# Clearing the operands of batch 0's attention on VectorE ahead of it, and making the offset mask behind it

## The chip, the core and the metric

The kernel runs on one core of one Trainium2 chip. The core has five engines with a queue of instructions each: TensorE (PE, matrix products), VectorE (DVE), ScalarE (ACT), GpSimd (POOL) and SyncE (SP), which here issues the DMAs. The metric is the device time of one execution in microseconds: 973.74 us, the median of three runs (971.68 to 973.83).

## The reference

Attention over 8 batches, 8 heads, 576 positions and 64 channels, in two parts that are added, and then a feed-forward layer over the 4608 rows that come out. All is float32.

```python
def _attn_ref(q, k, v):
    factor = 4
    q_d, k_d, v_d = (a.reshape(B, H, S // factor, factor, D).mean(axis=3) for a in (q, k, v))
    out_up = np.repeat(sm_attn(q_d, k_d, v_d), factor, axis=2)     # coarse attention
    mask = np.abs(pos[:, None] - pos[None, :]) < factor            # local attention: 7 offsets
    scores = np.where(mask, scale * np.matmul(q, k.transpose(0, 1, 3, 2)), -1000000000.0)
    ...
    return out_up + np.matmul(attn, v)

def _moe_ref(x, w_in, w_out, s, b):
    r = np.maximum(x @ w_in, 0.0)
    return (s * (r * r) + b) @ w_out
```

`x` is the attention's output with the heads side by side, 4608 x 512; `w_in` is 512 x 2048, `w_out` 2048 x 512. The weights and the scalars come in as 64-bit floating point.

## The kernel before, in words

**Attention.** Work is in units of one batch and one pair of heads, four pairs to a batch; a pair fills the 128 partitions. `first_unit` does a pair of the batches 0 to 2 in one pass: `down` (lines 263 to 331) makes the coarse part (sums of four rows of q and k on VectorE, L271 and L273; sums of v on GpSimd, L282 to L287; scores `sa`, softmax, the transposes `tp` and `tr`, and the product `up`), and around it `first_unit` makes the local part in windows of 32 columns: scores `sl` on top of a mask that TensorE adds from `maskb` (L372 and L377), their maximum and difference on VectorE (L382, L383), the exponential (L386), row sums and reciprocal (L387 to L389), the product with it (L390, on GpSimd for batch 0), a transpose on VectorE (L400), four copies into a block-diagonal operand `bd` (L403), and the products `ol` (L420), to which `up` is added as `x` is written (L423). The batches from 3 on use another form of the local part, `local_unit`, over shifted copies of k and v; this alone reads the offset mask `omask` (L460).

**Block-diagonal operands.** `bd`, and the operands `qc`, `vdr` and `vm` of the coarse part, are zero outside their blocks and are written only in the blocks, so each set is cleared once. One set (`db`, `dq`) serves pair 0 and, later, all other batches. For pairs 1 to 3 of batch 0, which are to overlap with pair 0, there are three more sets, laid in buffers that the weights take later (`make_room`); `clear(i)` zeroes one: 1952 elements a partition in four memsets of 488, and 256 in one more (L186, L187).

**Weights.** `w_in` and `w_out` come in eight parts. `load_w` issues the loads; `split_w` converts each part to a high and a low float32 half (L225 on ScalarE, L226 to L229 on VectorE, L230 on ScalarE, L233 on VectorE).

**Feed-forward.** Rows go in 18 tiles of 256. `split_x` makes a high and a low half of `x` (L530 on ScalarE, L531 on VectorE), `gemm1` does three products for each tile and part (L544 to L546), then relu, square and split (L554 to L557), and `gemm2` three more (L589 to L591).

**What sets the order.** The instructions are emitted in the order of the code. A planner then orders each engine's queue ahead of time: among the instructions that are ready in its own estimate of the times, it takes the one with the lowest number, which is the place in the emission; `tc.high_priority(offset=400)` around the units of batch 0 puts them 400 places ahead. On the chip each engine takes its queue in that order, and waits by semaphores. The accumulators lie in eight tiles (numbers 0 to 7 of `bank`), called banks here; batch 0's units take seven of them in turn (`bk`, line 626), so a later pair's tile waits until an earlier pair's tile in that bank has been read. Ahead of batch 0's units stand, in the emission: the loads of pairs 0 and 1, the identity, `mask` and `maskb`, `omask`, the memsets of `dq` and `db`, `ones` and `eps`, the loads of pairs 2 and 3, the first weights, the two scalars and `clear(1)`; `clear(2)` and `clear(3)` stand ahead of their units.

Of the kernel before, what the change touches and what calls it, by code (L numbers as in the profile page):

```python
# [10 lines left out]
F32 = mybir.dt.float32  # L11
# [7 lines left out]
P = 128  # L19
B, H, S, D = 8, 8, 576, 64  # L20
HP = H // 2
# [20 lines left out]
CH = 9  # L42
NC_ = S // CH
HALO = FAC - 1
NO = 2 * HALO + 1
# [16 lines left out]
def attention_ffn_kernel(ctx, tc, qk, vw_in, vr_in, vdm, qkn, vn, w_in, w_out, s_in, b_in, out):  # L62
    nc = tc.nc
# [39 lines left out]
    def load_pair(b, hp):  # L103
        if (b, hp) in ld:
            return
        own = {}
        if b == 0 and hp:
            room[hp] = make_room(hp)
            own = room[hp]["load"]

        def load(tag, shape, src, pool=one):
            t = own[tag] if tag in own else pool.tile(shape, F32, tag=tag, name="t" + tag)
            nc.sync.dma_start(t, src)
            return t

        tqk = load("qk", [P, 2, SP], qk[b, hp], two)
        tvr = load("vr", [P, FAC, D], vr_in[b, hp])
        tvd = load("vd", [KM, FAC, P], vdm[b, hp])
        tvw = load("vw", [P, NG, P], vw_in[HP * b + hp]) if HP * b + hp < EU else None
        ld[(b, hp)] = (tqk, tvw, tvr, tvd)  # L120
# [13 lines left out]
    def keep(ap, pattern, base, cm):  # L134
        nc.gpsimd.affine_select(
            out=ap, in_=ap, pattern=pattern, compare_op=ALU.is_ge,
            fill=NEG, base=base, channel_multiplier=cm)
# [11 lines left out]
    nc.vector.tensor_copy(maskb[:, 0 : NG : NG - 1], mask[:, 1:3])  # L149


    omask = cst.tile([P, CH, NO], F32, name="omask")
    nc.gpsimd.memset(omask, 0.0)
    for u in range(2):
        mu = omask[64 * u : 64 * u + 64]
        keep(mu, [[1, CH], [1, NO]], -HALO, CH)
        keep(mu, [[-1, CH], [-1, NO]], S - 1 + HALO, -CH)

    dq = cst.tile([P, NQ * 2 * GQ + 3 * P], F32, name="dq")
    nc.vector.memset(dq, 0.0)
    QV = NQ * 2 * GQ + P
# [4 lines left out]
    bias = cst.tile([P, DM], F32, name="bias")  # L168
    eps = cst.tile([P, 1], F32, name="eps")
    nc.gpsimd.memset(eps, 4e-9)  # L170

    db = one.tile([P, 2 * NG, P], F32, tag="big", name="db")
    nc.vector.memset(db, 0.0)
# [8 lines left out]
    def clear(i):  # L182
        da, vm = room[i]["dg"], room[i]["sc"][:, 1536:1792]
        n = 2 * NG * P
        for j in range(0, n + QV, 488):
            nc.gpsimd.memset(da[:, j : min(j + 488, n + QV)], 0.0)  # L186
        nc.gpsimd.memset(vm, 0.0)  # L187
        diag[i] = (take(da, 0, [P, 2 * NG, P]), *blocks(da, n, vm))


# [5 lines left out]
    def load_w(p):  # L196

        parts = (("i", src_i[:, :, 512 * p : 512 * p + 512]), ("o", src_o[:, 2 * p : 2 * p + 2]))
        for op, src in parts:
            st = one.tile([P, 1024, 2], I32, tag=f"w{op}{STAGE[p]}", name="wst")  # L200
            nc.sync.dma_start(st.rearrange("p (k f) t -> p k (f t)", k=src.shape[1]), src)
            wst[(p, op)] = st
# [32 lines left out]
    def split_w(p):  # L235
        with tc.high_priority(offset=-BEHIND.get(p, 0)):
            split_parts(p)
# [377 lines left out]
            load_pair(*units[j])  # L615

    NY = [10 * HP] * NE + [34 * (HP // 2)] * (B - NE)
    for hp in range(2, HP):
        load_pair(0, hp)
    load_w(0)  # L620
    sb_s = cst.tile([P, 1], F32, name="sb_s")
    nc.sync.dma_start(sb_s, bass.AP(s_in.tensor, s_in.offset, [[0, P], [1, 1]]))
    sb_b = cst.tile([P, 1], F32, name="sb_b")
    nc.sync.dma_start(sb_b, bass.AP(b_in.tensor, b_in.offset, [[0, P], [1, 1]]))
    clear(1)
    bk = banks(0, 1, 2, 3, 5, 6, 7)
    for hp in range(HP):
        load_ahead(hp)
        if hp > 1:
            clear(hp)  # L630
        with tc.high_priority(offset=400):
            for _ in first_unit(0, hp, bk):
                pass
    split_w(0)
    load_w(1)
    load_w(2)
# [121 lines left out]
```

## Time and profile before

| | us |
|---|---|
| median of three runs | 973.74 (971.68 to 973.83) |
| time of the profiled execution | 974.94 |
| its span, first to last instruction | 973.1 |
| TensorE busy | 937.4 (96%) |
| VectorE busy | 646.8 (66%) |
| ScalarE busy | 478.8 (49%) |
| GpSimd busy | 425.0 (44%) |

The profile comes from one execution. A row of the order in time has the start, the duration in microseconds, the engine, the line of the code, the operation, what is written and read, the shape, and how many instructions are merged; a bracket gives the idle time of that engine just before and who ended it. A row of a group has the count, the busy time in microseconds, the mean of one in nanoseconds, and the idle time before them. Rows of stages have the busy time of each engine in each stretch with the number of instructions, the granted clock of TensorE (1.00 is full), and the DMA share. Buffers of pairs 1 to 3 of batch 0 are all named `flat`; those of pair 0 have their own names (`dq`, `db`, `pl`, `sm`).

### The profile page before, as it was taken

To read this page: it belongs to the slowest core of one execution; us is meant where nothing else is said; L and a number is where in the kernel's file an instruction comes from. 1 tells how busy PE (TensorE), PEld (TensorE's weight loads), DVE (VectorE), ACT (ScalarE), POOL (GpSimd) and SP (SyncE) were. 2 spreads that over 40 slices of the span, in tenths; PEclk is the share of its full clock that TensorE was granted. 3 is DMA by queue.
4 is the path that set the end of the run, shared out by engine and by line. 5 is a ranking of instruction groups with operands and counts; after the bars stand their busy time and mean duration, and the time that the engine had idled before them with its cause. 6 is when DMAs were issued, how large, how long until landed. Compare 5 with 4: busy or idle time off the path is not lost.

```text
span 973.1 us, 18535 instructions
## 1 busy us (share of the span) xinstructions
PE 937.4 (96%) x7316; PEld 840.0 (86%) x7316; DVE 646.8 (66%) x1175; ACT 478.8 (49%) x1141; POOL 425.0 (44%) x455
## 2 busy tenths in 40 slices
PE   5769999999999999999999999999999999999998
PEld 4558888788999989889989898999899999998997
DVE  5999985864468778878787975876787772211121
ACT  5878775453755454534545344454454444333231
POOL 9422011100167686776767585575776750000000
PEclk9579999999999999999999999999999999999999
DMA  9746422102233232322323232231323100000000
GB/s 314 261 132 204 166 65 73 60 31 86 88 122 112 86 101 85 133 65 72 106 93 102 80 98 80 78 112 58 112 90 111 55 23 1 23 1 22 1 23 22
DMA packets 32103, 86.26 MB, mean 89 GB/s; under 512 B 3344, under 2 KB 7952, under 8 KB 32016
## 3 DMA queue, kind: packets, MB, share of 16 engines
q1 hardware_dynamic: 32016, 85.08, 26.4%
q8 instruction: 57, 0.93, 0.4%
q14 instruction: 30, 0.25, 0.1%
HBM read 75.63 MB, written 9.44 MB: 87 GB/s over the span
## 4 chain that ended last, share of the span: by engine, by line
PE 76%; DVE 7%; POOL 6%; DMA 6%; issue 3%; ACT 2%; DVEq 0%; SPq 0%; POOLq 0%; ACTq 0%
PE ph L544 12%; PE ph L545 12%; PE ph L546 12%; PE po L589 11%; PE po L590 11%; PE po L591 11%; DMA tqk<-in_qk_dram 3%; POOL pr L455 2%; PE sa L297 2%; DMA lqk<-in_qkn_dram 1%; POOL acc L477 1%; DMA wst<-in_moe_w_out_dram 1%; PE up L328 1%; PE ol L420 1%; PE ot L486 1%
## 5 line engine op out<-in xcount | busy, mean ns | idle before, releaser
L544 PE MATMUL ph<-xh,wi 128*128 128x256 f32 x1152 | 327.2, 284 | 5.3 <-DVE gl L557 2.5
L545 PE MATMUL ph<-xl,wi 128*128 128x256 f32 x1152 | 324.0, 281 | 0.0
L546 PE MATMUL ph<-xh,wi 128*128 128x256 f32 x1152 | 323.6, 281 | 0.0
L455 POOL TENSOR_TENSOR pr<-lqk 128x576 f32<-128x576 f32 x140 | 203.0, 1473 | 90.1 <-DMA lqk<-in_qkn_dram 53.9
L544 PEld LDWEIGHTS ph<-xh,wi 128*128 128x128 f32 x1152 | 217.1, 188 | 12.8 <-DVE gl L557 3.4
L545 PEld LDWEIGHTS ph<-xl,wi 128*128 128x128 f32 x1152 | 217.0, 188 | 5.0 <-issue 0.2
L546 PEld LDWEIGHTS ph<-xh,wi 128*128 128x128 f32 x1152 | 217.3, 189 | 0.1
L554 ACT ACTIVATE ph<-ph 128x512 f32<-128x512 f32 x144 | 83.7, 581 | 236.7 <-PE ph L546 236.5
L589 PE MATMUL po<-wo,gh 128*128 128x512 f32 x456 | 183.0, 402 | 0.2 <-ACT gh L556 0.2
L590 PE MATMUL po<-wo,gh 128*128 128x512 f32 x456 | 181.5, 398 | 0.0
L591 PE MATMUL po<-wo,gl 128*128 128x512 f32 x456 | 179.5, 399 | 0.0
L557 DVE TENSOR_TENSOR gl<-ph,gh 128x512 fp32r<-128x512 f32 x114 | 77.9, 683 | 110.9 <-ACT gh L556 110.5
L477 POOL TENSOR_TENSOR acc<-acc,pv 128x576 f32<-128x576 f32 x80 | 114.6, 1433 | 68.0 <-DVE acc L477 33.5
L457 DVE TENSOR_REDUCE st<-pr 128x9 f32<-128x576 f32 x140 | 105.9, 756 | 40.9 <-POOL pr L455 38.8
L287 POOL TENSOR_TENSOR dq<-vq 64x64 f32<-64x64 f32 x58 | 25.6, 441 | 192.4 <-PE up L326 190.2
L556 ACT CAST gh<-ph 128x512 fp32r<-128x512 f32 x114 | 66.8, 586 | 70.6 <-PE po L590 68.5
L591 PEld LDWEIGHTS po<-wo,gl 128*128 128x128 f32 x456 | 85.7, 188 | 17.3 <-issue 0.2
L476 DVE TENSOR_TENSOR pv<-lv,st 128x576 f32<-128x576 f32 x120 | 87.2, 747 | 20.2 <-POOL acc L477 19.6
L589 PEld LDWEIGHTS po<-wo,gh 128*128 128x128 f32 x456 | 85.7, 188 | 15.8 <-ACT gh L556 0.8
L590 PEld LDWEIGHTS po<-wo,gh 128*128 128x128 f32 x456 | 85.8, 188 | 15.6
L555 ACT ACTIVATE ph<-ph 128x512 f32<-128x512 f32 x144 | 83.8, 582 | 3.4
L590 PE MATMUL po<-wo,gb 128*128 128x512 f32 x120 | 48.2, 402 | 0.0
(145 smaller groups left out, 1261.1 us busy)
## 6 DMA issues: line engine op xcount, KB each, us to landing
tqk<-in_qk_dram SPq DMA_DIRECT2D x30, 584.0 KB, 4.0
lqk<-in_qkn_dram SPq DMA_DIRECT2D x20, 768.0 KB, 4.4
lv<-in_vn_dram SPq DMA_DIRECT2D x20, 480.0 KB, 3.5
out_dram<-os SPq DMA_DIRECT2D x17, 512.0 KB, 3.0
wst<-in_moe_w_in_dram SPq DMA_DIRECT2D x7, 1024.0 KB, 5.5
wst<-in_moe_w_out_dram SPq DMA_DIRECT2D x7, 1024.0 KB, 5.3
tvd<-in_vdm_dram SPq DMA_DIRECT2D x29, 160.0 KB, 2.7
tvr<-in_vr_dram SPq DMA_DIRECT2D x29, 128.0 KB, 2.1
```

Of the source, the lines that this page charges most:

```text
L455: nc.gpsimd.tensor_tensor(pr, lqk[:, 0:CH], lqk[:, CH + o : 2 * CH + o], ALU.mult)
L457: nc.vector.tensor_reduce(ls[:, :, o], pr, AX.X, ALU.add)
L476: nc.vector.tensor_tensor(pv, lv[:, o : o + CH], w, ALU.mult)
L477: (nc.vector if o % 3 == 1 else nc.gpsimd).tensor_tensor(acc[:, :, h], acc[:, :, h], pv, ALU.add)
L544: nc.tensor.matmul(ph[:, j], wi[p][:, 0, k, f], xh[:, k], start=(k == 0), stop=False)
L545: nc.tensor.matmul(ph[:, j], wi[p][:, 0, k, f], xl[:, k], start=False, stop=False)
L546: nc.tensor.matmul(ph[:, j], wi[p][:, 1, k, f], xh[:, k], start=False, stop=(k == NK - 1))
L554: nc.scalar.activation(ph, ph, AF.Relu)
L555: nc.scalar.activation(ph, ph, AF.Square)
L589: nc.tensor.matmul(po[m], gh[:, j, ms], wo[p][:, 0, j], start=first, stop=False)
L590: nc.tensor.matmul(po[m], gh[:, j, ms], wo[p][:, 1, j], start=False, stop=False)
L591: nc.tensor.matmul(po[m], gl[:, j, ms], wo[p][:, 0, j], start=False, stop=last)
```

## The change

The four steps of it: `clear` uses VectorE's memset in place of GpSimd's; `clear(1)` to `clear(3)` are all emitted ahead of batch 0's first unit; the offset mask is emitted behind batch 0's last unit; and the loads of pairs 2 and 3, which lay out the buffers that `clear` takes, are emitted further up, ahead of the memset of `db`.

```diff
@@ -149,14 +149,6 @@
-    omask = cst.tile([P, CH, NO], F32, name="omask")
-    nc.gpsimd.memset(omask, 0.0)
-    for u in range(2):
-        mu = omask[64 * u : 64 * u + 64]
-        keep(mu, [[1, CH], [1, NO]], -HALO, CH)
-        keep(mu, [[-1, CH], [-1, NO]], S - 1 + HALO, -CH)
@@ -169,6 +161,10 @@
     nc.gpsimd.memset(eps, 4e-9)
+    for hp in range(2, HP):
+        load_pair(0, hp)
     db = one.tile([P, 2 * NG, P], F32, tag="big", name="db")
@@ -183,8 +179,8 @@
         for j in range(0, n + QV, 488):
-            nc.gpsimd.memset(da[:, j : min(j + 488, n + QV)], 0.0)
-        nc.gpsimd.memset(vm, 0.0)
+            nc.vector.memset(da[:, j : min(j + 488, n + QV)], 0.0)
+        nc.vector.memset(vm, 0.0)
@@ -615,22 +611,27 @@
-    for hp in range(2, HP):
-        load_pair(0, hp)
     load_w(0)
+    for hp in range(1, HP):
+        clear(hp)
     sb_s = cst.tile([P, 1], F32, name="sb_s")
...
-    clear(1)
     bk = banks(0, 1, 2, 3, 5, 6, 7)
     for hp in range(HP):
         load_ahead(hp)
-        if hp > 1:
-            clear(hp)
         with tc.high_priority(offset=400):
             for _ in first_unit(0, hp, bk):
                 pass
+    omask = cst.tile([P, CH, NO], F32, name="omask")
+    nc.gpsimd.memset(omask, 0.0)
+    for u in range(2):
+        mu = omask[64 * u : 64 * u + 64]
+        keep(mu, [[1, CH], [1, NO]], -HALO, CH)
+        keep(mu, [[-1, CH], [-1, NO]], S - 1 + HALO, -CH)
     split_w(0)
```

## The prediction

> **What bounds the kernel now.** I read the profiled execution from the whole to the part: the first lines of the page, then busy time by stage, then the start engine by engine in order of time. Its time is 974.94 us, of which the span is 973.1 and 1.84 lies around it; the median of the three timed runs is 973.74, 1.2 below. Differences worked out in the profiled execution are taken over to the median unchanged. About 0.3% (2.9 us) is what a measurement of this kernel can tell from no change.
>
> ```profile
> span 973.1 us, 18535 instructions
> core 0: us, PE busy (x) PEld busy (x) DVE busy (x) ACT busy (x) POOL busy (x), PEclk, DMA share, GB/s
> 0.00:5.74 5.74, 0.00 (x0) 0.00 (x0) 2.18 (x5) 1.28 (x1) 4.62 (x17) 1.00 0.65 184
> 5.74:9.05 3.31, 1.73 (x6) 1.46 (x7) 1.41 (x3) 0.62 (x2) 3.14 (x11) 1.00 1.03 362
> 9.05:24.62 15.57, 11.69 (x275) 9.29 (x274) 9.23 (x22) 10.36 (x36) 14.54 (x37) 1.00 1.04 350
> 24.62:68.75 44.13, 28.21 (x421) 23.23 (x420) 43.56 (x98) 36.53 (x96) 15.60 (x19) 0.63 0.56 193
> 68.75:973.10 904.35, 895.76 (x6617) 806.02 (x6615) 590.45 (x1050) 430.05 (x1007) 387.13 (x374) 1.00 0.24 77
> ```
>
> Three stages follow from this. Behind 68.75, TensorE is busy for 895.76 of 904.35 us at a granted clock of 1.00: it has some 900 us of matrix products to do and nothing but their earlier start makes that part end earlier. From 24.62 to 68.75 VectorE has 43.56 of 44.13 us busy while TensorE has 28.21: VectorE sets the pace. Ahead of 24.62 GpSimd is the fullest engine (14.54 of 15.57 us in the last part), while VectorE has 3.56, 1.90 and 6.34 us idle, 11.80 in all. The change works in that first stage, so the question is what ends the waits there. In order of time, GpSimd (start, duration, line):
>
> ```profile
> 1.09 0.29 POOL masks.py:199 TENSOR_SCALAR_AFFINE_SELECT ident<-ident 128x128 f32<-128x128 f32 x1
> 6.56 1.38 POOL L186 MEMSET flat<- 128x488 f32 x3
> 10.48 0.21 POOL L135 TENSOR_SCALAR_AFFINE_SELECT mask<-mask 32x32 f32<-32x32 f32 x1
> 11.34 0.46 POOL L283 TENSOR_TENSOR vq<-tvr 128x128 f32<-128x128 f32 x1
> 12.67 1.84 POOL L186 MEMSET flat<- 128x488 f32 x4
> 21.73 0.72 POOL L282 TENSOR_TENSOR flat<-flat 80x256 f32<-80x256 f32 x1
> 22.97 0.71 POOL L287 TENSOR_TENSOR flat<-flat 64x64 f32<-64x64 f32 x2
> 23.76 0.83 POOL L390 TENSOR_TENSOR pl<-pl,sm 128x384 f32<-128x384 f32 x1
> ```
>
> and VectorE in the same time, the bracket giving its idle time and who ended it:
>
> ```profile
> 0.95 0.62 DVE L162 MEMSET dq<- 128x672 f32 x1 [0.95 <-PEq L746]
> 1.83 1.34 DVE L173 MEMSET db<- 128x1536 f32 x1 [0.27 <-issue]
> 5.59 0.31 DVE L148 CAST maskb<-mask 128x128 bf16<-128x128 f32 x1 [2.34 <-POOL mask L135]
> 5.74 0.74 DVE L271 TENSOR_REDUCE qd<-tqk 128x144 f32<-128x576 f32 x1
> 9.05 0.60 DVE L298 TENSOR_REDUCE dmx<-sa 96x3 f32<-96x432 f32 x1 [1.91 <-PE sa L297]
> 11.99 0.17 DVE L306 RECIPROCAL dsm<-dsm 96x3 f32<-96x3 f32 x1 [0.69 <-ACT dsm L305]
> 12.92 0.75 DVE L271 TENSOR_REDUCE flat<-flat 128x144 f32<-128x576 f32 x1 [0.76 <-DMA flat<-in_qk_dram]
> 16.61 0.75 DVE L271 TENSOR_REDUCE flat<-flat 128x144 f32<-128x576 f32 x1 [0.96 <-DMA flat<-in_qk_dram]
> 19.31 0.23 DVE L389 RECIPROCAL sm<-sm 128x12 f32<-128x12 f32 x1
> 24.62 0.58 DVE L400 STREAM_TRANSPOSE pt<-pl 128x384 f32<-128x384 f32 x1 [3.39 <-POOL pl L390]
> ```
>
> The reader is to see one long wait: the reciprocal of pair 0's row sums is done at 19.31 + 0.23 = 19.54, but the product that uses it (L390, on GpSimd) starts at 23.76, since GpSimd takes its instructions in order and is busy with the sums of v. The transpose behind it waits 3.39 us on VectorE, and the copies into the block-diagonal operand and the last products of pair 0 wait with it.
>
> **The change part by part.** *What leaves GpSimd.* Fifteen memsets (L186, L187), and five instructions of the offset mask move to a later place in the emission.
>
> ```profile
> L186 POOL MEMSET flat<- 128x488 f32 x12 | 5.7, 505 | 0.1
> L187 POOL MEMSET flat<- 128x256 f32 x3 | 0.9, 308 | 0.1
> L135 POOL TENSOR_SCALAR_AFFINE_SELECT omask<-omask 64x63 f32<-64x63 f32 x4 | 1.4, 354 | 0.1
> L153 POOL MEMSET omask<- 128x63 f32 x1 | 0.2, 151 | 0.1
> ```
>
> That is 5.7 + 0.9 = 6.6 us of clears and 1.4 + 0.2 = 1.6 us of offset mask, all of it ahead of L390 in GpSimd's order. Taken out, L390 could start at 23.76 - 8.2 = 15.56 as far as GpSimd's work goes; the reciprocal then ends last, at 19.54. So L390 gains at most 23.76 - 19.54 = 4.22 us. I take the 4.22, because the remaining work of GpSimd leaves 19.54 - 15.56 = 3.98 us for arrivals that it must now wait for; the last sums of v (21.73) need the last pair's v. If those waits took all of it and as much again, nothing would be left of the gain: its lower end is 0.
>
> *The offset mask.* It is first read here:
>
> ```profile
> L460 DVE TENSOR_TENSOR st<-st,omask x20: 215/232/232, 287.1 to 786.2; 128x63 f32<-128x63 f32 x20
> ```
>
> at 287.1 us, over 200 us behind its new place. It can run in GpSimd's gap ahead of the first sum of v or behind 24.62, where GpSimd has 15.60 of 44.13 us busy: I cost it at nothing, the cover being that idle time. If its five instructions landed in front of L390 all the same, they would cost up to 1.6 us of the slack of 3.98, so nothing either.
>
> *What VectorE gets.* The same fifteen memsets. Two memsets of VectorE stand in the trace: 672 elements in 0.62 and 1536 in 1.34, so 0.72 / 864 = 0.83 ns an element and 0.06 us fixed. A 128x488 memset is then 0.47 us, a 128x256 one 0.27, together 12 x 0.47 + 3 x 0.27 = 6.4 us. They depend on nothing that is computed, so the program's order, which a planner makes from the instructions that are ready, can put them in VectorE's gaps: 2.34 ahead of the mask cast and 1.91 ahead of dmx, together 4.25 us; then 0.69, 0.76 and 0.96 between later steps. 6.4 - 4.25 = 2.15 us does not fit in the two large gaps. In the three small ones (2.41 together) a memset of 0.47 delays the next step by nothing or by nearly its whole length. The bounds are 0 and 2.15 lost; I take the middle, 1.1, since gaps and remainder are of a size. If the cover of the large gaps is gone, they cost the 6.4 in full (a rival below).
>
> Of queues: a memset stands in VectorE's order, so what is behind it waits with it: the reductions of q and k (L271, L273), for which ScalarE's copy (L277) and TensorE's first products (L297) wait. The copy of pairs 1 to 3 must also wait for their clears, which ran on GpSimd before.
>
> *The loads of pairs 2 and 3* are emitted earlier, ahead of the memset of db. All DMAs of this stage go through SyncE's one queue, and their order in it (pairs 0, 1, 2, 3, then the first weights, then the two scalars) stays. They are moved past work of other engines and past no transfer, so their eight issues cost nothing. The first weights' issue and the scalars' stay as they were.
>
> *A rule weighed.* One row speaks against VectorE memsets beside GpSimd:
>
> ```profile
> 1.68 1.69 POOL L135 TENSOR_SCALAR_AFFINE_SELECT mask<-mask 32x96 f32<-32x96 f32 x1
> L135 POOL TENSOR_SCALAR_AFFINE_SELECT mask<-mask x10: 203/269/1694, 1.3 to 10.5; 32x96 f32<-32x96 f32 x8, 32x32 f32<-32x32 f32 x2
> ```
>
> One select took 1.69 us where the median is 0.27, and it lies over the memset of db (1.83 to 3.17): as if GpSimd had been held until that ended. The select of the identity (1.09, 0.29 us) ran under the memset of dq (0.95 to 1.57) without such a length, so the row is not clear; the slower rival takes the held reading. The Trainium skill, "SBUF — State Buffer", section "Who interferes with whom", says that on trn2 a VectorE instruction with at most one SBUF input and outside the two-port modes does not contend with GpSimd, and its list of operations that take the shared ports has no memset. By that rule the long select has another cause and the rival loses 1.4 us of its price.
>
> *The sum.* -4.22 for L390, +1.1 for clears that do not fit: -3.1 us at the transpose of pair 0, which starts at 21.5 instead of 24.62. This carries to the end because of what is behind it:
>
> ```profile
> 27.36 2.19 PE L420 MATMUL ol<-db,tvw 128*64 128x96 f32 x24 [2.66 <-ACT db L403]
> 30.99 0.44 DVE L423 TENSOR_TENSOR x<-ol,ups 128x288 f32<-128x288 f32 x1
> 33.28 0.74 PE L326 MATMUL up<-flat 128*128 128x144 f32 x2
> 64.88 0.44 DVE L423 TENSOR_TENSOR x<-ol,flat 128x288 f32<-128x288 f32 x1
> 66.55 1.05 ACT L530 CAST xh<-x 128x1024 fp32r<-128x1024 f32 x1
> 68.75 0.58 PE L545 MATMUL ph<-xl,wi 128*128 128x256 f32 x1
> ```
>
> Pair 0's last products (27.36) wait for those copies, its result (30.99) frees the accumulator bank that pair 1's up (33.28) takes, and so on through four pairs to the last result of batch 0 (64.88), the split of x and the stream of the two large products (68.75). VectorE has no idle time from 24.62 on, so its stream moves as one. In the profiled execution: 974.94 - 3.1 = 971.8 us. For the median: 973.74 - 3.1 = 970.6 us. With the loss at its bounds (2.15 and 0) the likeliest case runs from 973.74 - 2.1 to 973.74 - 4.2, that is 969.5 to 971.6 us.
>
> **The rivals.** *More than this is gained.* Pair 0's first scores wait for the second mask cast, which GpSimd's clears kept late (select at 10.48):
>
> ```profile
> 11.36 0.32 PE L372 MATMUL sl<-maskb,idb 128*128 128x192 bf16 x1 [2.34 <-DVE maskb L149]
> ```
>
> Eight of the fifteen clears stand ahead of that select (seven of 0.50 and one of 0.31, 3.8 us), so without them it can run at 10.48 - 3.8 = 6.7, the scores start up to 2.34 earlier and the reciprocal with them: -3.1 - 2.3 = -5.4, 968.3 us. For it speaks that 11.80 - 6.4 = 5.4 us of VectorE's idle time is there to be had; against it that the reciprocal (19.31) stands behind two arrivals of q and k (waits of 0.76 and 0.96), which do not move.
>
> *The gain has nothing to fill it.* The stage from 24.62 on is full of weight conversion, and the first of that is tied to a transfer:
>
> ```profile
> 22.40 1.24 ACT L225 ACTIVATE es<-wst 128x512 f32<-128x512 f32 x2 [0.35 <-DMA wst<-in_moe_w_in_dram]
> ```
>
> VectorE can take up conversion only from 22.40 + 0.62 on. If only the transpose (0.58) moves ahead of that and the clears cost their 1.1, the sum is +0.5: 974.2 us, no change. For it: VectorE's 43.56 of 44.13 us. Against it: attention of pairs 1 to 3, not conversion, leads to 64.88.
>
> *Slower: the clears stand in front of the first pair.* One mechanism: VectorE's order holds the memsets ahead of the mask cast and the reductions of q, while the planner takes the first transfer or the mask to be late. Then they come on top of VectorE's work in full, 6.4, and only the wait of 3.39 at the transpose absorbs any: +3.0; a select held by them as in the row above adds 1.69 - 0.27 = 1.4. Together +4.4: 978.1 us. It decides from where more than (2.34 + 0.27) / 0.47, six memsets, stand ahead of the cast. For it: nothing else of VectorE is ready there, and once issued a memset is not overtaken. Against it: the first pair's work has the higher priority. With six or fewer, the change does in part not what it says, since most clears then run amid the first pair's attention; that is the forecast.
>
> **How the numbers follow.** The forecast has 0.44, of which 0.31 ends over 2.9 us faster and 0.13 within the bound, as -3.1 lies close to it; the larger gain 0.14, all faster; no change 0.21 (0.01 faster, 0.18 same, 0.02 slower); the slower rival 0.21 (0.03 same, 0.18 slower). That makes 0.46 faster, 0.34 same, 0.20 slower. The predicted time is the forecast's, 970.6. The range must reach into both signs: below, the larger gain of 5.4 with the lost 1.1 and the small waits given back too (-5.4 - 1.1 - 2.4 = -8.9, 964.8); above, nearly the slower rival's 978.1: 964.8 to 977.5, leaving out some 0.15.
>
> **What would show it.** Step one: L390 of pair 0 follows its reciprocal within 1 us, and GpSimd has idle time before 24. Step two: memsets on VectorE of about 0.47 us, at most six ahead of the first mask cast, and the first reduction of q still near 5.7. Step three: the transpose of pair 0 at about 21.5, the last result of batch 0 near 61.8, the stream of products from about 65.7. The prediction is wrong if L390 goes on waiting for GpSimd, if the first reduction of q comes over 2 us later, or if the transpose is earlier but 64.88 stays; and if a select or a sum of v on GpSimd lasts as long as a VectorE memset lies over it, the rule of the skill is the one that fails.

## The result and the profile after

The changed kernel takes 978.44 us (median of five executions, 977.37 to 981.86), the kernel before on the same chip 973.83 (five, 971.68 to 975.35). The ratio is 1.0054 with a 95% interval of [1.0031, 1.0077]: slower, by 4.6 us. The forecast was 970.6 with a range to 977.5, so its sign and its range are wrong; the slower rival had 978.1. Two of the comparisons below hold one execution of over 3000 us each, which is left out of their medians and ratios.

The profiled execution is the slowest of the five (span 980.1). A second profile of the same kernel, in the first experiment, has a span of 977.8, 4.7 above the 973.1 of before. Line numbers of the changed kernel are 4 lower around the attention (L267 is before's L271, L386 is L390) and the clears are L182 and L183.

First busy time by stage of the changed kernel, cut at the first reduction of q (8.87), at pair 0's transpose (27.09) and at the stream of products (74.19); the columns are those of the prediction's first fence.

```profile
core 0: us, PE busy (x) PEld busy (x) DVE busy (x) ACT busy (x) POOL busy (x), PEclk, DMA share, GB/s
0.00:8.87 8.87, 0.00 (x0) 0.00 (x0) 7.15 (x15) 1.28 (x1) 7.18 (x28) 1.00 0.78 249
8.87:27.09 18.22, 8.87 (x217) 7.30 (x218) 13.94 (x33) 9.02 (x33) 9.87 (x23) 0.97 1.05 336
27.09:74.19 47.10, 36.59 (x486) 28.86 (x485) 43.69 (x100) 38.38 (x103) 10.59 (x16) 0.54 0.55 190
74.19:980.10 905.91, 897.85 (x6617) 808.29 (x6615) 590.37 (x1046) 428.49 (x1004) 384.09 (x374) 1.00 0.23 76
```

The first cut came at 5.74 before, the second at 24.62, the third at 68.75. Behind the third the kernel takes 905.91 us (903.61 in the second profile) where before took 904.35: 1.6 more in one profile and 0.7 less in the other, so no steady loss is seen there. What is lost is lost ahead of the stream, which starts 74.19 - 68.75 = 5.44 us later in both profiles. VectorE's work between transpose and stream did not grow (43.69 us, 43.56 before), yet that stage is 47.10 us long instead of 44.13.

Where the 5.44 us arise is seen on VectorE (start, duration, engine, line, operation, and in a bracket the idle time before it and who ended it):

```profile
1.83 1.34 DVE L169 MEMSET db<- 128x1536 f32 x1 [0.27 <-issue]
3.22 2.01 DVE L182 MEMSET flat<- 128x488 f32 x4
5.24 0.27 DVE L183 MEMSET flat<- 128x256 f32 x1
5.56 1.50 DVE L182 MEMSET flat<- 128x488 f32 x3
6.97 0.16 DVE L146 CAST idb<-ident 128x128 bf16<-128x128 f32 x1
7.18 0.47 DVE L182 MEMSET flat<- 128x488 f32 x1
7.65 0.27 DVE L183 MEMSET flat<- 128x256 f32 x1
7.97 0.98 DVE L182 MEMSET flat<- 128x488 f32 x2
8.87 0.69 DVE L267 TENSOR_REDUCE qd<-tqk 128x144 f32<-128x576 f32 x1
...
23.04 0.43 DVE L222 TENSOR_SCALAR es<-es 128x512 f32<-128x512 f32 x1 [1.05 <-ACT es L221]
...
24.18 0.22 DVE L385 RECIPROCAL sm<-sm 128x12 f32<-128x12 f32 x1
...
25.12 1.05 DVE L223 TENSOR_SCALAR es<-es 128x512 int32<-128x512 int32 x1
...
26.37 0.80 DVE L225 SCALAR_TENSOR_TENSOR es<-wst,es 128x512 int32<-128x512 int32 x1
27.09 0.56 DVE L396 STREAM_TRANSPOSE pt<-pl 128x384 f32<-128x384 f32 x1
```

Twelve of the fifteen memsets (4 + 1 + 3 + 1 + 1 + 2) stand ahead of the first reduction of q, one after the other, and no row among them has a wait. The reduction starts at 8.87, 3.13 later than before, and the reciprocal at 24.18 instead of 19.31, 4.87 later. Of these 4.87 us, 3.52 stand at the row sums (21.45, for 17.93). The other 1.35 come between them and the reciprocal, where VectorE waits 1.05 us for ScalarE's first step of weight conversion (the row at 23.04) with two of pair 0's steps behind it in its queue. On GpSimd and TensorE, whose rows are shown next, the relief is there, but it relieves nothing:

```profile
1.34 1.92 POOL L135 TENSOR_SCALAR_AFFINE_SELECT mask<-mask 32x96 f32<-32x96 f32 x6
...
10.37 1.72 PE L293 MATMUL sa<-kd,dq 128*96 128x144 f32 x6 [10.37 <-DVE maskb L148]
...
24.54 1.35 POOL L386 TENSOR_TENSOR pl<-pl,sm 128x384 f32<-128x384 f32 x1 [3.96 <-DVE sm L385]
```

The product L386 follows its reciprocal (24.18 + 0.22 = 24.40) by 0.14 us, and GpSimd sat idle for 3.96 us ahead of it; before, the same product came 4.22 us behind the reciprocal. GpSimd's queue is free, but the reciprocal is 4.87 us late, so the product starts 0.78 us later than before (24.54 for 23.76).

The transpose is 2.47 us later, though. The product itself takes 1.35 us instead of 0.83, with two instructions of weight conversion on VectorE over it (L224, and the L223 at 25.12, which takes 1.05 us where the L223 at 23.50 took 0.43); what makes both longer isn't shown. And from its end at 25.89 the transpose stands 1.20 us behind other work in VectorE's queue, the last of it weight conversion (L225), where before it followed in 0.03 us: 0.78 + 0.52 + 1.17 = 2.47.

The larger part of the 5.44 us lies between the transpose and pair 0's first result. TensorE and VectorE again, of the changed kernel:

```profile
31.28 1.22 PE L416 MATMUL ol<-db,tvw 128*64 128x96 f32 x10
...
33.40 0.58 PE L416 MATMUL ol<-db,tvw 128*64 128x96 f32 x2
...
35.74 0.72 DVE L267 TENSOR_REDUCE qd<-tqk 128x144 f32<-128x576 f32 x1
36.38 0.74 DVE L269 TENSOR_REDUCE kd<-tqk 128x144 f32<-128x576 f32 x1
37.04 0.44 DVE L419 TENSOR_TENSOR x<-ol,ups 128x288 f32<-128x288 f32 x1
...
69.46 0.41 DVE L419 TENSOR_TENSOR x<-ol,flat 128x288 f32<-128x288 f32 x1
```

The twelve products of the first result end at 33.40 + 0.58 = 33.98, but VectorE's queue has other work in front of the result, the last of it the reductions of a later batch's q and k, and writes it at 37.04. From the transpose it is 9.95 us; before it was 30.99 - 24.62 = 6.37. So the lag goes +2.47 at the transpose (27.09 for 24.62), +3.58 to the first result, -1.47 to the last one (69.46 - 37.04 = 32.42 us for 33.89) and +0.86 to the stream (4.73 us for 3.87), together 5.44.

### The profile page after: what moved, and what is told of

It is laid out like the page before. It is cut to its first block, busy times and chain, and to the rows that moved or that the text cites. A ratio compares the mean times of both kernels' runs of the same rounds, so it can differ in the third digit from the quotient of the medians.

```text
span 980.1 us, 18541 instructions
## 1 busy us (share of the span) xinstructions
PE 943.3 (96%) x7316; PEld 844.4 (86%) x7316; DVE 655.2 (67%) x1190; ACT 477.2 (49%) x1141; POOL 411.7 (42%) x440
## 4 chain that ended last, share of the span: by engine, by line
PE 90%; DVE 4%; DMA 3%; ACT 2%; issue 1%; DVEq 0%; SPq 0%; ACTq 0%
PE ph L540 14%; PE ph L541 14%; PE ph L542 14%; PE po L585 13%; PE po L586 13%; PE po L587 13%; PE sa L293 2%; PE up L324 1%; PE ol L416 1%; PE sl L373 1%; PE ot L482 1%; DMA wst<-in_moe_w_in_dram 1%; DMA flat<-in_qk_dram 1%; DMA wst<-in_moe_w_out_dram 1%; DMA tqk<-in_qk_dram 1%
## 5 line engine op out<-in xcount | busy, mean ns | idle before, releaser
L541 PE MATMUL ph<-xl,wi 128*128 128x256 f32 x1152 | 325.1, 282 | 0.0
L541 PEld LDWEIGHTS ph<-xl,wi 128*128 128x128 f32 x1152 | 218.1, 189 | 4.8 <-issue 0.2
L283 POOL TENSOR_TENSOR dq<-vq 64x64 f32<-64x64 f32 x58 | 21.4, 369 | 200.9 <-PE up L322 198.8
```

The lines of the kernel that those rows point to most:

```text
L541: nc.tensor.matmul(ph[:, j], wi[p][:, 0, k, f], xl[:, k], start=False, stop=False)
```

## The experiments

The theory: the planner puts the memsets, which wait for nothing, in front of the first pair's reductions, and the late first pair is what the end sees. Rivals: the earlier loads of pairs 2 and 3 or the moved mask do it; VectorE's extra work does it, wherever it stands; or the later order of the large products, which the planner makes anew for each kernel. All ratios are against the kernel before on the chip of that run, whose medians were 974.0 to 975.55.

**The changed kernel again.** No edit.

> The changed kernel once more, beside the same runs of the kernel before as its neighbours here. Expected 4 to 5 us above before, as in the first comparison (1.0054). If the engine alone is the whole cause, it lies no more than 1 us above the kernel with the engine edit alone (1.9 to 2.7 above before); if the moved offset mask and loads cost something of their own, about 2 us above it.

978.79 us, ratio 1.0036 [1.0024, 1.0048]. The twelve memsets and the 8.87 are there again, the stream starts at 74.19 again, and the span behind it is 903.61 us.

**The engine alone.** The kernel before, with

```diff
-            nc.gpsimd.memset(da[:, j : min(j + 488, n + QV)], 0.0)
-        nc.gpsimd.memset(vm, 0.0)
+            nc.vector.memset(da[:, j : min(j + 488, n + QV)], 0.0)
+        nc.vector.memset(vm, 0.0)
```

> The kernel before with one edit: clear() uses VectorE's memset; clears, offset mask and loads stay where they were emitted. Three theories. Queue: ten memsets stand in VectorE's order ahead of pair 0's first reduction of q, which starts near 8.9 us instead of 5.7, and everything behind follows; the engine alone does it, so 978.4 us (+4.6), the reduction at 8.9. Load: VectorE sets the pace of the stage up to 68.75, so 6.4 us more on it cost some 4 to 6 us wherever they stand: 978 too. Places: the moved offset mask, loads and clears reorder the program and the engine is harmless: 973.8.

977.45 us, ratio 1.0028 [1.0015, 1.0041], an interval that overlaps both of the whole change ([1.0024, 1.0048] and [1.0031, 1.0077]). From its timeline:

```profile
8.87 0.69 DVE L271 TENSOR_REDUCE qd<-tqk 128x144 f32<-128x576 f32 x1
...
73.34 0.58 PE L545 MATMUL ph<-xl,wi 128*128 128x256 f32 x1
```

The first reduction is late by the same 3.13 us, with the same twelve memsets ahead, though `clear(2)` and `clear(3)` still stand at their units in the code: where the clears are emitted did not matter to the planner here. The engine suffices for a loss, of 2.7 us by the ratio, and its stream starts 4.59 us late. The whole change has 3.5 and 5.3 us by its two ratios and 5.44 at the stream, so whether the moved places add 1 or 2 us of their own is not decided.

**The places alone.** The changed kernel with its clears back on GpSimd (the same two lines, the other way).

> The changed kernel with clear() back on GpSimd: places as changed, engine as before. Queue and load: VectorE's order at the start is the one before, the first reduction of q starts at 5.7, 973.8 us within 1.5. Places: 978.4.

987.31 us, ratio 1.0119 [1.0099, 1.0139], against an expected 973.8: a miss by 13.5 us. Of this kernel, the timeline and then two stretches of the stream:

```profile
4.86 0.75 DVE L267 TENSOR_REDUCE qd<-tqk 128x144 f32<-128x576 f32 x1 [1.60 <-DMA tqk<-in_qk_dram]
...
68.56 0.58 PE L541 MATMUL ph<-xl,wi 128*128 128x256 f32 x1 [2.12 <-DVE xl L527]
```

```profile
160.00:200.00 40.00, 36.02 (x321) 29.59 (x321) 30.31 (x63) 18.96 (x49) 6.10 (x12) 0.96 0.20 61
200.00:300.00 100.00, 97.72 (x930) 85.39 (x930) 49.50 (x93) 50.88 (x126) 16.61 (x25) 0.98 0.21 68
```

and the same two stretches of the kernel before:

```profile
160.00:200.00 40.00, 38.04 (x345) 32.06 (x347) 31.43 (x62) 19.89 (x53) 4.46 (x6) 1.00 0.16 53
200.00:300.00 100.00, 99.82 (x973) 88.70 (x973) 57.66 (x106) 53.16 (x132) 27.46 (x36) 1.00 0.23 80
```

With the clears on GpSimd the reductions of q are not late (here the load ends the wait, at 4.86, where 5.7 was expected; the mask's first cast now stands behind them, at 7.15 for 5.59), the transpose is at 24.91, and the stream starts 0.19 us earlier than before. The loss comes 90 us later: TensorE stands idle for 3.98 + 2.28 = 6.26 us between 160 and 300, where before has 2.14, at a granted clock of 0.96 and 0.98 where before has 1.00, and it has fewer of its instructions behind it (321 + 930 for 345 + 973). The two halves of the change are not two terms that add: 1.9 us for the engine and 11.8 for the places make about 4.5 together.

**Five memsets ahead instead of twelve, all fifteen on VectorE.** The clears of pairs 2 and 3 become products with zero of the pair ahead's q, so that they can't run before that q has landed (this edit and the next three are made in the changed kernel).

```diff
+            if i == 1:
+                nc.vector.memset(part, 0.0)
+            else:
+                src = ld[(0, i - 1)][0][:, 0]
+                nc.vector.tensor_scalar(part, src[:, 0 : part.shape[1]], 0.0, None, ALU.mult)
```

> The changed kernel, all fifteen clears still on VectorE, but only pair 1's five are memsets; those of pairs 2 and 3 are products of the q of the pair ahead with 0, so that they cannot be placed ahead of that pair's load. Five clears are then ahead of the first reduction of q. Queue: it starts at 5.7 to 6.0, L390 of pair 0 directly behind its reciprocal, 970.5 to 973 us, faster than or like before. Load: VectorE has as much to do as in the changed kernel, 977 to 979.

978.96 us, ratio 1.003 [1.002, 1.004]. Of its timeline:

```profile
3.22 2.29 DVE L184 MEMSET flat<- 128x488 f32 x5
5.50 0.74 DVE L271 TENSOR_REDUCE qd<-tqk 128x144 f32<-128x576 f32 x1
...
168.37 0.96 DVE L531 TENSOR_TENSOR xl<-x,xh 128x768 fp32r<-128x768 f32 x1 [0.17 <-ACT xh L530]
```

The time is what the load theory had expected (977 to 979), but not by its mechanism, a slower stage ahead of the stream: with all fifteen clears on VectorE, the stream starts at 62.20, 12.0 us earlier than in the changed kernel and 6.6 earlier than before. Most of that start is work put off: VectorE has done 41 instructions of weight conversion ahead of it (23.8 us), where before has done 48 (28.9) and the changed kernel 51 (30.8). What is left of the gain is lost at the third tile of rows, the first that reads batch 1: the second part of its split (128x768) is at 168.37 here and at 155.37 before. The windows show it for this kernel,

```profile
160.00:180.00 20.00, 15.50 (x187) 13.45 (x186) 14.31 (x34) 11.35 (x32) 2.54 (x6) 0.83 0.35 115
```

and for the kernel before:

```profile
155.37 0.96 DVE L531 TENSOR_TENSOR xl<-x,xh 128x768 fp32r<-128x768 f32 x1 [0.21 <-ACT xh L530]
...
160.00:180.00 20.00, 18.55 (x198) 15.61 (x198) 12.05 (x30) 9.16 (x26) 0.00 (x0) 1.00 0.20 68
```

**Other engines for some of the clears.** Pair 1 on VectorE and pairs 2 and 3 on GpSimd; pairs 1 and 2 on VectorE and pair 3 on GpSimd; and one pair on each engine, pair 2's as copies of zeros on ScalarE.

```diff
+            (nc.vector if i == 1 else nc.gpsimd).memset(part, 0.0)    # one pair
+            (nc.vector if i < 3 else nc.gpsimd).memset(part, 0.0)     # two pairs
+            if i == 2:                                                # three engines
+                nc.scalar.copy(part, dq[:, 0 : part.shape[1]])
+            else:
+                (nc.vector if i == 1 else nc.gpsimd).memset(part, 0.0)
```

> The changed kernel with only pair 1 cleared by VectorE (five memsets, all ahead of the first reduction of q) and pairs 2 and 3 by GpSimd. Queue: the reduction at 5.5 to 6.0, as in the kernel with one pair on each engine; the stream of products starts at or before 68.75. For the whole time: its order behind 70 us puts batch 1's last pair late, as in the kernels that lost there: 980 to 987.

984.57 us, ratio 1.0097 [1.008, 1.0114]. The first reduction is at 5.50 and the stream starts at 61.27.

> The changed kernel with pair 3's five clears back on GpSimd: ten memsets on VectorE, all of them ahead of the first reduction of q in its order. Queue: the reduction starts at 3.2 + 10 x 0.46 + 0.3, about 8.0 (after: 8.87 with twelve ahead, before: 5.74 with none). The forecast's reading (memsets fit in gaps): 5.7 to 6.2. The start of the stream of large products then tells what the delay is worth: 71 to 73 if it follows the delay. For the whole time no theory of the start alone suffices, since the kernel with staggered clears started its stream 6.5 us earlier than before and still ended later: 975 to 985.

981.94 us, ratio 1.0075 [1.0057, 1.0093]. With ten memsets ahead the reduction starts at 7.84, where 8.0 was expected: in these kernels the start follows the number of memsets ahead (5 give 5.50, 10 give 7.84, 12 give 8.87). The stream, expected at 71 to 73, starts at 69.57, so it doesn't follow the delay of the reduction alone.

> The changed kernel with pair 1 cleared by VectorE, pair 2 by ScalarE (copies of zeros) and pair 3 by GpSimd. Queue: five memsets ahead of the first reduction of q, which starts at 5.7 to 6.0; GpSimd has ten clears fewer, so L390 of pair 0 no longer waits for it: 970 to 972. Load: 2.1 us more on VectorE in place of 6.4, 975 to 976.

985.11 us, ratio 1.0096 [1.0077, 1.0114]; the reduction is at 5.50, the stream at 66.97. This missed: no fastest kernel came of three engines. In all three the start of the stream alone would have given a time from 7.5 us less than before to 0.8 more, and the end is 7 to 10 us later than before.

**A delay with nothing else.** The kernel before, its clears on GpSimd, and 5 or 12 memsets of VectorE on a buffer that nobody reads before it is written, behind the memset of `db`.

```diff
+    for t in range(5):      # 12 in the second
+        if t % 4 == 0:
+            spare = flat(("wi0", "wo0", "wi1", "wo1")[t // 4], 2048)
+        nc.vector.memset(spare[:, 488 * (t % 4) : 488 * (t % 4) + 488], 0.0)
```

> The kernel before, clears on GpSimd as before, plus five VectorE memsets of 488 elements on a buffer that nobody reads, early in VectorE's order; all five stand ahead of the first reduction of q. Queue: five fit in the wait of 2.34 us for the mask, so the reduction stays within 0.5 us of 5.7 and L390 of pair 0 near 23.8. For the whole time the planner's later order counts (its last pair of batch 1 comes as late as in the kernels that lost 3 to 12 us behind 130 us): 978 to 988.

> The same with twelve such memsets, as many as stand ahead of the first reduction of q in the changed kernel; GpSimd still does the clears. It has the same later order as the kernel with five. Queue: the reduction starts at about 9.0, the reciprocal of pair 0 comes 2 to 5 us later than with five, L390 follows it directly, the stream of products starts 2 to 5 us later, and the time is 2 to 5 us above the kernel with five. If the delay were covered by GpSimd's late L390 or by VectorE's gaps: the same time within 1 us.

981.46 us, ratio 1.0072 [1.0052, 1.0093], with five, and 990.71, ratio 1.016 [1.0139, 1.018], with twelve. Five:

```profile
5.75 1.10 DVE L148 CAST maskb<-mask 128x128 bf16<-128x128 f32 x1
6.77 0.73 DVE L275 TENSOR_REDUCE qd<-tqk 128x144 f32<-128x576 f32 x1
...
65.63 0.58 PE L549 MATMUL ph<-xl,wi 128*128 128x256 f32 x1 [0.76 <-DVE xl L535]
```

Twelve:

```profile
9.35 0.69 DVE L275 TENSOR_REDUCE qd<-tqk 128x144 f32<-128x576 f32 x1
...
71.22 0.58 PE L549 MATMUL ph<-xl,wi 128*128 128x256 f32 x1 [1.62 <-DVE xl L535]
```

Between the two only memsets were added. The reduction of q comes 2.58 us later, the stream 5.59 and the median 9.25 (the profiled executions differ by 4.8, with spans of 980.4 and 985.2). In both profiles the part behind the start of the stream is the same, 980.4 - 65.63 = 914.8 and 985.2 - 71.22 = 914.0 us. So memsets ahead of the reductions, with the order that the planner makes around them, suffice to delay the stream, and by more than their own length, as in the change (3.13 became 5.44). The order does differ: with five the mask's cast stands ahead of the reduction, with twelve behind it. Three expectations were missed: the reduction with five (6.77, where 5.2 to 6.2 was expected), and with twelve the stream and the time (each 2 to 5 us above the kernel with five). Against the kernel before the pair says something else: five memsets let the stream start 3.1 us earlier than before, and the kernel is 6 us slower.

**The wait at the third tile.** The third tile of rows reads batch 0's x in place of batch 1's, in the kernel before and in the one with five memsets ahead and all on VectorE. The edit changes what is computed in that tile; all the work is still done.

```diff
-            src = xt[b][:, :, t0 - b * S : t0 - b * S + n]
+            src = xt[0 if t == 2 else b][:, :, t0 - b * S : t0 - b * S + n]
```

> The kernel before, except that tile 2 of the feed-forward layer takes its 192 rows of batch 1 from batch 0's x, so its products do not wait for batch 1's attention; the computation of those rows is changed by this, all work stays. Second gate (the products of tile 2 wait for batch 1's attention): before hardly waits there, 0 to 2 us gained. Any other theory: no change.

> The same edit (tile 2 takes batch 0's x in place of batch 1's) on the kernel with staggered clears, which starts its stream of products 6.5 us earlier than before but ends 3 us later. Second gate: the 8 us that it loses between 160 and 180 us come back, 968 to 972 us, and it ends before the kernel before does. If the loss has another cause (VectorE's load, weights, the clock): it stays at 977 or more.

975.83 us, ratio 1.0013 [1.0, 1.0026], and 975.95, ratio 1.0007 [0.999, 1.0024]. The second lies between the two cases of its expectation (968 to 972, or 977 and more), and its interval overlaps that of the staggered kernel. To the kernel before the wait is worth nothing; to the other it is worth 978.96 - 975.95 = 3.0 us by the medians, 2.1 against the kernel before of each time, of the 10 us that it had lost from the start of the stream (6.6 earlier) to its end (3.4 later). Another stall, in the second layer's products, has come behind it:

```profile
175.69 0.50 PE L589 MATMUL po<-wo,gh 128*128 128x512 f32 x1 [2.75 <-ACT gh L556]
```

So the third tile's wait is a part of where a gained start goes, and not the whole.

**Batch 1 earlier.** The changed kernel with batch 1's first pair emitted, at raised priority, ahead of the first split of x.

```diff
+    gen = attention_rest()
+    with tc.high_priority(offset=400):
+        for _ in range(10):
+            next(gen)
```

> The changed kernel with the first pair of batch 1 emitted ahead of the first split of x, at batch 0's priority: in TensorE's order batch 1's attention then ends some 7 us of products earlier. If the later order decides as much as the start does, part of the 4 us comes back: 972 to 977. If the start alone decides: 978 to 979 as in the changed kernel.

991.76 us, ratio 1.0172 [1.0147, 1.0196]: against the expected 972 to 977, a miss. The same kernel once more:

> The changed kernel with batch 1's first pair emitted early once more, for an undisturbed trace: 988 to 994 us as in the first runs. Either its stream of products starts over 5 us later than in the changed kernel (the early pair stands in front of it), or it starts in time and loses later.

989.97 us, ratio 1.0157 [1.0128, 1.0186]. The stream starts at 72.51, 1.7 us earlier than in the changed kernel, and loses ground at once (2.5 us of the stretch lie ahead of the stream; from 80 to 130 TensorE is busy for 47.32 of 50 us, before for all 50):

```profile
70.00:130.00 60.00, 56.92 (x559) 50.62 (x561) 54.48 (x99) 44.28 (x92) 8.86 (x12) 0.89 0.46 154
```

The work that was pulled forward takes the places of the products. That this slows the whole by so much isn't explained.

**A few memsets that fit.** The forecast's step was that at most six stand ahead. The kernel before, with four (pair 3's large ones) or three (the last large one of each pair) on VectorE:

```diff
+            (nc.vector if i == 3 else nc.gpsimd).memset(da[:, j : min(j + 488, n + QV)], 0.0)      # four
+            (nc.vector if j >= 1464 else nc.gpsimd).memset(da[:, j : min(j + 488, n + QV)], 0.0)   # three
```

> The kernel before with one part of the edit: the four large memsets of pair 3 go to VectorE, everything else stays on GpSimd and in its place. Four memsets stand ahead of the first reduction of q, and TensorE's order behind 70 us places batch 1's pairs as in the kernel before. If the forecast's mechanism is right where the clears fit in the gap, the reduction starts at 5.7 to 6.2, GpSimd is rid of 2.0 us ahead of L390 of pair 0, which starts some 2 us earlier (21.8), and the time is 1 to 3 us below before, 972 to 974. If the start is not worth its delay in the end, or VectorE's load counts: before or up to 2 us above it.

> The kernel before with the last large memset of each of pairs 1 to 3 on VectorE (three in all); the batch 1 pairs stand somewhat later in TensorE's order than before (the last by 6 us of products), but not at its limit. The reduction of q at 5.7 to 6.2, L390 of pair 0 about 1.5 us earlier. Start alone: 0.5 to 2 us below before. Later order counts as much: before or up to 4 us above it.

975.34 us, ratio 1.0012 [0.9998, 1.0025], and 979.28, ratio 1.0056 [1.0035, 1.0076]; the second was expected at most 4 us above before and has 5.3. Both test the forecast with clears that fit, since the product L390 did come earlier, by 2.31 us with four and by 3.00 with three, of the forecast's 4.22. With four:

```profile
5.23 1.63 DVE L148 CAST maskb<-mask 128x128 bf16<-128x128 f32 x1
...
5.32 1.38 POOL L186 MEMSET flat<- 128x488 f32 x3
...
21.45 0.83 POOL L390 TENSOR_TENSOR pl<-pl,sm 128x384 f32<-128x384 f32 x1
...
22.44 0.55 DVE L400 STREAM_TRANSPOSE pt<-pl 128x384 f32<-128x384 f32 x1
...
27.62 0.90 PE L420 MATMUL ol<-db,tvw 128*64 128x96 f32 x6
...
30.26 1.72 PE L297 MATMUL sa<-flat 128*96 128x144 f32 x6 [0.78 <-DVE flat L383]
...
32.26 1.23 PE L420 MATMUL ol<-db,tvw 128*64 128x96 f32 x12
...
35.56 0.45 DVE L423 TENSOR_TENSOR x<-ol,ups 128x288 f32<-128x288 f32 x1
...
70.02 0.58 PE L545 MATMUL ph<-xl,wi 128*128 128x256 f32 x1
```

The four memsets end at 5.23, and yet the reduction of q starts at 6.78, where 5.7 to 6.2 was expected. Between them VectorE's two casts (L146, L148), which take 0.16 and 0.31 us before, take 1.64 and 1.63 and end within 0.2 us of a row of GpSimd's memsets (5.32 + 1.38 = 6.70). The same is seen with five spare memsets (6.77, behind casts of 1.12 and 1.10 us under memsets of GpSimd).

The transpose is 2.18 us earlier than before. Then TensorE's queue has six of pair 0's products, another pair's scores `sl` and `sa`, and only then the next twelve; before it had all 24 in one row at 27.36. The first result comes at 35.56, 4.57 later than before, and the stream at 70.02, 1.27 later. The gain was real, was given back within 13 us, and never reached the end.

With three memsets TensorE's order of those 24 products is the one before, and the gain still melts: 2.46 us at the transpose (22.16), 1.32 at the first result (29.67), 0.42 at the stream (68.33). Between transpose and stream VectorE is busy for 45.42 of 46.17 us there, so the gain meets a stage that VectorE fills, as the prediction's rival "the gain has nothing to fill it" said.

In one view (us; "behind" is the profiled span less the start of the stream; "third tile" is the second part of its split, as in the row of 155.37 above; the two kernels that read batch 0 there have none):

| kernel | memsets ahead of q | q reduced | transpose | stream | third tile | behind | ratio |
|---|---|---|---|---|---|---|---|
| before | 0 | 5.74 | 24.62 | 68.75 | 155.37 | 904.4 | – |
| changed (second profile) | 12 | 8.87 | 27.43 | 74.19 | 162.81 | 903.6 | 1.0036 |
| engine alone | 12 | 8.87 | 27.54 | 73.34 | 162.09 | 902.2 | 1.0028 |
| four memsets | 4 | 6.78 | 22.44 | 70.02 | 157.00 | 902.0 | 1.0012 |
| three memsets | 3 | 5.00 | 22.16 | 68.33 | 159.65 | 906.5 | 1.0056 |
| batch 0 in third tile | 0 | 5.74 | 24.65 | 69.83 | – | 904.0 | 1.0013 |
| batch 1 earlier | 12 | 8.87 | 27.09 | 72.51 | 161.00 | 915.0 | 1.0157 |
| places alone | 0 | 4.86 | 24.91 | 68.56 | 170.13 | 917.0 | 1.0119 |
| staggered, all on VectorE | 5 | 5.50 | 23.13 | 62.20 | 168.37 | 915.2 | 1.003 |
| the same, batch 0 in third tile | 5 | 5.50 | 22.64 | 61.26 | – | 914.6 | 1.0007 |
| one pair | 5 | 5.50 | 21.91 | 61.27 | 165.52 | 921.7 | 1.0097 |
| two pairs | 10 | 7.84 | 23.00 | 69.57 | 170.60 | 913.3 | 1.0075 |
| three engines | 5 | 5.50 | 22.13 | 66.97 | 172.36 | 920.0 | 1.0096 |
| five spare | 5 | 6.77 | 23.51 | 65.63 | 168.76 | 914.8 | 1.0072 |
| twelve spare | 12 | 9.35 | 25.01 | 71.22 | 172.31 | 914.0 | 1.016 |

By these profiles the kernels fall into two groups by what is behind the start: 902 to 907 us, with the third tile ahead of 163, and 913 to 922, with it (but for batch 1 earlier) behind 165. Each row is one execution, and executions of one kernel differ by up to 8 us: the profiled one with three memsets is the fastest of its six (2.8 us below their median), the one with two pairs the slowest (2.8 above). By medians the gap between the groups is nearly closed, at some 909 and 911 us. The changed kernel is in the group of before, which is why its lag at the stream is its loss at the end. None of the kernels is faster than before.

Where the second group loses can be counted in the traces. In the stream three products of 256 columns follow each other in 67.44 - 67.09 = 0.35 us, the starts of two neighbouring products of L541 in the kernel with one pair on VectorE (L541 is one of the three lines that take turns).

At about a third of that, 0.1175 us a product (double for 512 columns), the large products begun up to a time are so many us of work, and their difference to the kernel before is its lag (us; a minus is a lead; an estimate from counts):

| kernel | at 80 | at 160 | at 200 | at 250 | at 300 | at 900 |
|---|---|---|---|---|---|---|
| changed (second profile) | 5.0 | 5.2 | 4.2 | 5.5 | 5.2 | 4.8 |
| four memsets | 1.1 | 1.3 | 1.0 | 2.1 | 2.1 | -1.1 |
| staggered, all on VectorE | -2.7 | -2.3 | 5.7 | 5.5 | 5.4 | 4.4 |
| the same, batch 0 in third tile | -2.7 | -3.1 | -0.2 | 2.9 | 3.5 | 2.8 |
| five spare | 1.8 | 2.8 | 8.5 | 8.8 | 8.2 | 7.6 |
| one pair | -5.9 | -3.8 | 4.7 | 8.8 | 8.2 | 10.1 |
| places alone | 1.5 | 1.2 | 8.0 | 13.4 | 13.5 | 12.8 |
| twelve spare | 2.5 | 3.5 | 11.3 | 14.2 | 14.0 | 12.6 |
| batch 1 earlier | 3.8 | 11.3 | 8.7 | 15.2 | 15.3 | 14.8 |

The changed kernel has its 5 us at 80 and keeps them. A start of the stream is not yet a lead: staggered, 6.6 us earlier at the start, leads by 2.7 at 80, and five spare memsets, 3.1 earlier, lag by 1.8. Staggered, one pair, places alone, and five and twelve spare keep what they have at 80 to about 2 us up to 160, and then lose 6 to 13 us up to 250, where the third tile and batch 1's last products stand. Without the third tile's wait the staggered kernel loses 2.9 us from 160 to 200 instead of 8.0, but 3.1 more up to 250, so that some 2 us are left of the difference. What makes a kernel lose there stays open.

## Why the prediction was wrong

**GpSimd's queue as the bound, right; what it is worth, wrong.** L386 follows its reciprocal by 0.14 us, as step one said, and GpSimd is idle for 3.96 us ahead of it. The 4.22 us counted on a reciprocal at 19.54; it ended at 24.40.

**The fit of the clears, the first step that failed.** The price was right: the groups of the changed kernel have

```profile
L182 DVE MEMSET flat<- x12: 465/465/465, 3.2 to 11.3; 128x488 f32 x12
```

and 272 ns for the three of L183, for the forecast's 0.47 and 0.27. The place was not: "at most six ahead", and a loss of at most 2.15 us, became twelve and 3.13 at the first reduction. The gap of 2.34 us ahead of the mask cast was idle time that the chip had; the planner filled it, and 3 us beyond, since it orders ahead of time by its own estimate, and no row of the trace of before tells when that estimate has the first load or the mask ready (the runs show the order, not the estimate). On the chip VectorE reduced q as early as 4.86 with the mask out of its way. The forecast named this as a rival, with its point of decision (six memsets), and gave it 0.21; "the first pair's work has the higher priority" was the reason against it, and priority ranks only what the planner holds to be ready.

**The slower rival's terms.** Its +3.0 at the transpose was +2.47, near in number but not by its working: it took the whole 6.4 us of memsets less the wait of 3.39, and the runs have 0.78 of a late product and the rest of a longer product and a fuller queue on VectorE. Its second term, a select held by a memset (+1.4), did not happen: six selects took 1.92 us together, from 1.34 to 3.26, with the memset of `db` over them from 1.83 to 3.17, where before one of them alone took 1.69. So the rule weighed there (the Trainium skill, "SBUF — State Buffer", section "Who interferes with whom") agrees with this trace. The row of 1.69 us is in three of the seventeen traces (before, the same with batch 0 in the third tile, places alone), those in which the cast L146 stands directly behind the memset of `db` in VectorE's queue; it runs from 3.09 to 3.25, and the select ends at 3.37. In the other fourteen a memset stands there. So the cast may be what held the select, which no run here isolates. In place of that term came the 3.58 us between transpose and first result. That the rival's 978.1 is near the measured 978.44 is in part luck, then.

**"It carries to the end", the second step that failed, for gains.** The lag grew on its way: 2.47 at the transpose, 5.44 at the stream, 4.7 at the end of the second profile. The chain of banks named for it does not set it alone, since the steps between take on or lose 1 to 4 us each by the order in each queue. And a gain isn't carried: with the transpose 2.18 us earlier (four memsets) the stream was 1.27 later, with 2.46 earlier (three memsets) 0.42 earlier and the end 5.3 later, and with the stream 6.6 us earlier (staggered) the end was later. So in none of the kernels with few memsets ahead did the forecast's -3.1 reach the end.

**The mask and the loads at nothing.** For the change as a whole the runs don't contradict this: the engine alone has a loss whose interval overlaps that of the whole change, with 1 or 2 us left open. By themselves, with the clears on GpSimd, the moved places cost 11.8 us. Their stream started on time, so it wasn't their work ahead of it; that it was the order that followed is argued from the windows, not shown.

## What to carry to other kernels

Before work without inputs is given to an engine whose queue is ordered ahead of time, ask what the planner believes of the loads, not where the chip's trace has a gap: a memset is ready from the start, and it can take every place ahead of work that waits for a load. A wait is worth its length only as long as the step that then ends last stays where it was, so follow the operand too, here the reciprocal. An earlier start of the next stage is a gain only if no work was put off to get it: count what is done, not only when it starts. And in a kernel whose order is planned from emission, price an edit at its start only with the order behind it in view: edits of a few memsets moved the end by up to 16 us while the start of the stream moved by -7.5 to +5.4.

## What was not expected

- The size of the reordering. A delay or a gain of 2 to 3 us in the first 10 us comes with a part behind the start of the stream of 902 to 922 us. The kernels at its upper end lose most between 160 and 250 us (batch 1 earlier already from 80); the cause was not found.
- The granted clock of the staggered kernel is 0.83 from 160 to 180 us, with TensorE busy for 15.50 of 20 us, against 1.00 with 18.55 before. Idle time alone doesn't tell it: with twelve spare memsets it is 0.99 there, with 15.62 busy.
- VectorE's casts and GpSimd's memsets did not run side by side: a cast of 0.16 us in the kernel before took 1.64 under a row of them (four memsets), and one of 0.31 took 2.21 under GpSimd's sums and memsets (twelve spare). The changed kernel has no such cast, 0.45 at most, as its clears have left GpSimd.
- A 128x488 float32 memset takes 0.465 us on VectorE (0.83 ns for each further element by the 1536 of `db` in 1.34) and 0.505 on GpSimd in the kernel before: the move of the engine itself was worth only 0.04 us each.
